# Linear attention with slots and a gated MLP: the middle chunk's products with states in the other quarters of the array, behind the first link; the first expert layer's blocks in the order of use

## The chip, the cores and the metric

The kernel is one program on one core of one Trainium2 chip. The core has a matrix engine (TensorE; PE in the profile, its weight loads PEld), a vector engine (VectorE, DVE), a scalar engine (ScalarE, ACT), a third elementwise engine (GpSimd, POOL) and a sync engine (SP) that issues most transfers. Each works through its own instructions in order, and they wait for one another by semaphores. Matrix products land in PSUM, here in banks of 512 float32 numbers for each of 128 partitions; all other data stand in SBUF.

The metric is the device time of one run in microseconds (us). Before the change the median of three runs is 389.02 us (388.72 to 393.24).

## What is computed

Three layers follow each other: a linear attention with decay, a soft mixture of experts with 32 slots, and a gated MLP.

```python
for t in range(S):                                   # B, H, S, D = 4, 8, 768, 48
    state = alpha[:, :, t, :, None] * state + np.einsum('bhd,bhe->bhde', k[:, :, t], v[:, :, t])
    y[:, :, t] = np.einsum('bhd,bhde->bhe', q[:, :, t], state)
...
logits = x @ phi                                     # x: 3072 x 384, 32 slots
slot_input = softmax(logits, axis=0).T @ x
slot_out[e] = np.maximum(slot_input[e] @ w1[e], 0.0) @ w2[e]      # 8 experts, 384 -> 1024 -> 384
x = softmax(logits, axis=1) @ slot_out
...
g = x @ w_gate                                       # 384 -> 1536 -> 384
out = (g * sigmoid(g) * (x @ w_val)) @ w_out
```

## The kernel before

**The attention.** The 768 positions of a pair of heads (a unit; there are 16) are cut into six chunks of 128. A step works on half a unit, so there are 32 steps g = 0 to 31; h = g % 2 tells the half, c = 0, 1, 2 the chunk in it. The two heads stand in partitions 0 to 63 and 64 to 111. I call a step with h = 1 long and one with h = 0 short, after their times in the profile. A step of the loop in `fast` (L628 on) issues, for the matrix engine and in this order:

- the first link (`emit_st`, L402): the state at a chunk's end is the scaled sum of the chunk's own contribution and the state before. The matrix engine adds the earlier state to the contribution in PSUM by a product with the identity, and the scalar engine scales the sum and writes the state to SBUF (L404);
- the masked scores of the next half (`emit_s`, L353), then the second link, the transposes of the next half's keys (`emit_kt`, L371) and of the last half's output x (`emit_xt`, L462), and the logits of the last half (`emit_l`, L453);
- the products of this half's queries with the earlier states (`emit_past`, L420), into the bank `y`. A half with h = 0 has them for two chunks, since its first chunk has no state behind it, and a half with h = 1 for three;
- the next half's own contributions to the states (`emit_dh`, L390), into a bank of the pool `m`; where a unit begins, the scalar engine then scales the first of them (the state after chunk 0, `emit_st(g + 1, 0)`);
- the products of this half's values with its masked scores (`emit_ip`, L432), added to the same bank `y`, which one scalar copy (L434) brings to SBUF as x.

Each product is two matmul instructions. Those of the two heads stand in different parts of the array: in `emit_past` head 0 reads partitions 0 to 63 and writes partitions 0 to 63, head 1 reads and writes 64 to 111, so that two of the four quarters of the array are in use.

The vector engine makes the decay scans (L307, L314) and the mask of one head (L360), converts parts of a float64 weight to float32 (L253, L257, L261), and runs the short softmax parts of `slot_steps`. GpSimd scales keys and queries (L325) and masks the other head (L363). The scalar engine does the copies out of PSUM.

**The expert layers.** 32 blocks of 768 KB, 16 for each of the two layers, are fetched whole. `Arena` hands out SBUF columns, `loads` sets the order, and `pump` starts the next load when a place is free; in the attention a credit of `RATE` columns a step holds it back. The first layer (L853) runs over four groups: three slices k of the contraction, four experts e. A block before holds one expert's half, all three slices, so each block of a group is released near its end. The second layer is `fc2` (L910), 16 times eight matmuls, each on one block.

**The rest.** `c_stack`, `sw_mul`, `sw_sel` prepare the gated MLP, which runs 72 steps of eleven 512-wide matmuls (L1006, L1007, L1045).

Of the kernel before, what the change touches and what calls it, by code (L numbers as in the profile page):

```python
# [18 lines left out]
CH = 128  # L19
# [15 lines left out]
GV0, RATE = 1, 840  # L35
TINY = 2.0 ** -55
NEAR, ROUND = 31600, 19184
# [55 lines left out]
def attention_slots_mlp(ctx: ExitStack, tc: tile.TileContext, kq, at, vt, phi, w1, w2, wgv, wo, cst, out):  # L93
# [13 lines left out]
    phs = const.tile([112, NU, NSL], F32, name="phs")  # L107
# [33 lines left out]
    def program(general):  # L141
# [16 lines left out]
        zn = {nm: [0] * n for nm, n in (("a", 4), ("p", 5), ("v", 4), ("w", 2), ("x", 2))}  # L158
        zsize = {"a": HW, "p": HB, "v": 288, "w": HW, "x": 384}
        for z in "a0 a1 p2 a2 p3 v0 w0 a3 p4 v1 w1 p0 v2 p1 v3 x0 x1".split():  # L160
            zn[z[0]][int(z[1])] = ar.alloc(zsize[z[0]], 1)
# [32 lines left out]
        for q in range(2):  # L194
            loads += [("w1", (e, hf)) for hf in range(2) for e in range(4 * q, 4 * q + 4)]
# [6 lines left out]
        reserve = [0]  # L202
# [22 lines left out]
        def pump(limit=100):  # L225
            while loads and limit:
                limit -= 1
                nm, i = loads[0]
                o = ar.alloc(size[nm], 0 if nm == "wo" or loads[0] in lasts else 1 if ar.near(BLK) <= reserve[0] else None)
# [150 lines left out]

        def emit_dh(g):
# [4 lines left out]
            dps[g] = psm()  # L386
# [4 lines left out]

        dps = {}
# [15 lines left out]
        yps = {}  # L408


        def emit_past(g):
            n, h = sgs[g]
            q = view(qp[g], 112)
            yps[g] = ps_y.tile([128, 512], F32, tag="y", name="y")
            for c in range(3):
                cc = 3 * h + c
                o = slice(c * CH, (c + 1) * CH)
                for s in range(2) if cc else ():
                    p = slice(0, 64) if s == 0 else slice(64, 112)
                    nc.tensor.matmul(yps[g][p, o], lhsT=gst[n, cc][p, 0:p.stop - p.start], rhs=q[p, o], start=(cc == max(1, 3 * h)), stop=False, skip_group_check=True)  # L420
            del qp[g]
            release(pair.pop(g), z_p, g + 5)

        def emit_ip(g):
            n, h = sgs[g]
            v = view(vv[g]).rearrange("p (c e) -> p c e", e=96)
            ps = yps[g]
            for c in range(3):
                o = slice(c * CH, (c + 1) * CH)
                for s in range(2):  # L430
                    p = slice(0, 64) if s == 0 else slice(64, 112)
                    nc.tensor.matmul(ps[p, o], lhsT=v[:, c, 48 * s:48 * s + p.stop - p.start], rhs=smk[g, s][:, c], start=False, stop=True, skip_group_check=True)  # L432
            xt[g] = (z_x.pop(0), 384)
            nc.scalar.copy(view(xt[g], 112), ps[0:112, 0:384])  # L434
            del smk[g, 0], smk[g, 1], yps[g]
            release(vv.pop(g), z_v, g + 4)
# [8 lines left out]
        def emit_l(g):  # L445
# [5 lines left out]
            for j in range(3):  # L451
                t0 = j * CH
                nc.tensor.matmul(lps[b][32 * j:32 * j + 32, CH * h:CH * h + CH], lhsT=phs[:, u, :], rhs=x[:, t0:t0 + CH], start=(u == 0 and h == 0), stop=(u == NU - 1), skip_group_check=True)  # L453
# [14 lines left out]
        def slot_steps(b):  # L468
# [33 lines left out]

            def part(between=lambda: None):
# [3 lines left out]
                for r in range(2):  # L507
                    if r:
                        between()
                    for u, p, w in pieces:  # L510
                        for j in range(3):
                            nc.tensor.matmul(ps[32 * j:32 * j + 32, 96 * u:96 * u + 96 * w], lhsT=st["et"][:, r, 32 * j:32 * j + 32], rhs=xtok[:, p:p + w, 3 * r + j, :], start=(r == 0 and u == 0), stop=(r == 1), skip_group_check=True)
# [64 lines left out]
        def fast():  # L577
# [14 lines left out]
            keep_warm(10)  # L592
# [15 lines left out]
            keep_warm(4)  # L608
# [10 lines left out]
            keep_warm(6)  # L619
            pend = []  # L620
            credit[0] = 0
            for g in range(NSG):
                n, h = sgs[g]
                nxt = g + 1 < NSG

                emit_st(g, 1 - h)
                if GV0 < g and (g <= 8 or g % 8 not in (3, 4)):
                    conv_y()  # L628
# [22 lines left out]
                if g:  # L651
                    emit_l(g - 1)
                    release(xt.pop(g - 1), z_x, g + 1)
# [7 lines left out]
                emit_past(g)  # L661
# [13 lines left out]
                credit[0] = min(credit[0] + RATE, 2 * BLK)  # L675
# [6 lines left out]
                pump_units()  # L682
            for r in z_t:
# [498 lines left out]
```

## Time and profile before

One profiled execution took 390.72 us, 1.70 us above the median of the runs; its span from the first to the last instruction is 389.0 us. The stages, cut at instructions of the matrix engine, with the busy time of each engine in them:

| stage | from : to, us | PE | DVE | ACT | POOL | DMA, GB/s |
|---|---|---|---|---|---|---|
| start, steps 0 and the beginning of 1 | 0 : 16.98 | 12.11 | 12.66 | 4.42 | 6.45 | 312 |
| attention | 16.98 : 156.06 | 136.63 | 121.12 | 82.33 | 88.29 | 317 |
| last softmax, slot inputs | 156.06 : 162.48 | 5.75 | 2.13 | 2.77 | 0 | 275 |
| first expert layer | 162.48 : 175.63 | 13.15 | 1.91 | 4.76 | 2.55 | 354 |
| second expert layer | 175.63 : 188.88 | 11.59 | 9.14 | 4.02 | 3.55 | 410 |
| preparation of the MLP | 188.88 : 199.24 | 10.36 | 7.69 | 6.26 | 0 | 246 |
| gated MLP | 199.24 : 389.00 | 181.76 | 136.54 | 96.67 | 0 | 55 |

A row of the timeline in the prediction reads: start in us from the span's first instruction, length in us, engine, line, operation, what is written <- what is read, partitions and shape, number of instructions merged; in brackets the idle time of the engine ahead of it and who ended it. A matmul's end is modelled, so stages are measured from start to start. In the rows of waits stand the waiting engine and tile, the one waited for, the total in us, how often, and the longest.

### The profile page before, as it was taken

What the parts mean: (1) busy time and instruction counts of PE and PEld (TensorE: products, weight loads), DVE (VectorE), ACT (ScalarE), POOL (GpSimd) and SP (SyncE); (2) the same over time, 40 slices, a digit from 0 to 9 for tenths busy, and PEclk for the clock granted to TensorE, in tenths of its full rate; (3) what the DMA queues carried; (4) which work ended last, traced back from release to release, by engine and by line L of the source; (5) the groups of instructions that cost most, each with busy time, mean ns of one, the idle gap of its engine ahead of it and who ended that gap; (6) DMA issues with size and microseconds to landing.
All of it is one profiled execution on the core that took longest, in us unless ns stands there. A gap on an engine that the chain in (4) does not pass through costs nothing.

```text
span 389.0 us, 8609 instructions
## 1 busy us (share of the span) xinstructions
PE 371.4 (95%) x3308; PEld 278.9 (72%) x3309; DVE 291.2 (75%) x566; ACT 201.2 (52%) x468; POOL 100.8 (26%) x105
## 2 busy tenths in 40 slices
PE   7799999999999999899899999999999999999992
PEld 3577777777777776434368868888888888888881
DVE  6969997999999973215789987677777867877550
ACT  2256665666456565523376755445455545446441
POOL 3347875685588641010300000000000000000000
PEclk9879999999999999999999999999999999999998
DMA  8969999899899959899900004204204114112002
GB/s 273 352 221 329 373 352 356 289 340 345 275 346 363 336 164 354 298 345 412 401 30 0 3 27 125 73 3 150 71 2 153 40 33 152 37 36 82 3 1 90
DMA packets 28627, 74.25 MB, mean 191 GB/s; under 512 B 3216, under 2 KB 11648, under 8 KB 28576
## 3 DMA queue, kind: packets, MB, share of 16 engines
q1 hardware_dynamic: 28256, 73.27, 53.3%
q8 instruction: 28, 0.46, 0.5%
q10 hardware_dynamic: 272, 0.21, 0.2%
q14 instruction: 23, 0.19, 0.2%
q0 software_dynamic: 48, 0.13, 0.1%
HBM read 68.87 MB, written 4.72 MB: 189 GB/s over the span
## 4 chain that ended last, share of the span: by engine, by line
PE 81%; DVE 6%; DMA 3%; ACT 2%; issue 2%; POOL 1%; SPq 0%; DVEq 0%; ACTq 0%; POOLq 0%
PE m L1045 22%; PE acc L1045 11%; PE s L353 6%; PE y L432 6%; PE y L420 6%; PE s L1006 4%; PE m L402 4%; PE s L1007 4%; PE m L390 3%; PE m L371 3%; PE l L453 3%; DMA near<-w 3%; PE s L853 3%; PE m L462 2%; DVE near L1012 1%
## 5 line engine op out<-in xcount | busy, mean ns | idle before, releaser
L1045 PE MATMUL m<-rnd 128*128 128x512 f32 x432 | 129.2, 389 | 0.0
L1045 PEld LDWEIGHTS m<-rnd 128*128 128x128 f32 x432 | 81.1, 188 | 16.8
L1009 ACT ACTIVATE near<-s 128x512 f32<-128x512 f32 x72 | 43.1, 599 | 79.0 <-PE s L1006 77.3
L1045 PE MATMUL acc<-rnd 128*128 128x512 f32 x216 | 81.1, 392 | 0.7 <-DVE rnd L901 0.7
L325 POOL TENSOR_TENSOR far<-far 112x384 f32<-112x384 f32 x61 | 74.5, 1240 | 8.8 <-DVE far L307 4.7
L1012 DVE TENSOR_TENSOR near<-near,s 128x512 f32<-128x512 f32 x72 | 49.3, 685 | 36.1 <-ACT near L1009 35.9
L1020 DVE TENSOR_TENSOR rnd<-near,rnd 128x512 fp32r<-128x512 f32 x72 | 49.4, 686 | 3.2 <-ACT rnd L1018 3.1
L1045 PEld LDWEIGHTS acc<-rnd 128*128 128x128 f32 x216 | 40.5, 188 | 10.3 <-DVE rnd L901 1.6
L1018 ACT CAST rnd<-near 128x512 fp32r<-128x512 f32 x72 | 44.3, 616 | 0.2 <-DVE near L1012 0.2
L404 ACT ACTIVATE far<-m,tots 112x48 f32<-112x48 f32 x80 | 24.3, 304 | 26.7 <-PE m L402 14.6
L307 DVE TENSOR_TENSOR_SCAN far<-far,r 112x388 f32<-112x388 f32 x32 | 30.8, 962 | 5.1 <-DMA far<-at 2.4
L353 PE MATMUL s<-far 64*128 64x128 f32 x384 | 30.8, 293 | 3.5 <-POOL far L325 2.2
L363 POOL TENSOR_SCALAR_AFFINE_SELECT far<-far 128x384 f32<-128x384 f32 x32 | 20.2, 631 | 47.3 <-ACT far L362 47.3
L1116 DVE TENSOR_REDUCE amm<-near 112x1 f32<-112x768 f32 x32 | 30.3, 946 | 2.5 <-DMA near<-at 2.5
L314 DVE TENSOR_TENSOR_SCAN far<-far,r 112x387 f32<-112x387 f32 x32 | 30.7, 959 | 1.1
L257 DVE SCALAR_TENSOR_TENSOR near<-near 128x384 uint32<-128x384 uint32 x36 | 21.6, 599 | 11.3 <-ACT near L249 10.3
L434 ACT COPY far<-y 112x384 f32<-112x384 f32 x32 | 15.3, 480 | 28.3 <-PE y L432 28.3
L353 PEld LDWEIGHTS s<-far 64*128 64x128 f32 x384 | 24.7, 191 | 6.1 <-POOL far L325 4.5
L432 PE MATMUL y<-far 128*48 128x128 f32 (+1 forms) x384 | 28.9, 276 | 0.0
L1006 PE MATMUL s<-rnd 128*128 128x512 f32 x72 | 28.3, 393 | 0.0
L1007 PE MATMUL s<-rnd 128*128 128x512 f32 x72 | 28.1, 391 | 0.0
L420 PE MATMUL y<-far 48*48 48x128 f32 (+1 forms) x320 | 24.9, 283 | 0.0
(163 smaller groups left out, 493.4 us busy)
## 6 DMA issues: line engine op xcount, KB each, us to landing
near<-w SPq DMA_DIRECT2D x18, 768.0 KB, 7.3
far<-kq SPq DMA_DIRECT2D x32, 384.0 KB, 5.1
far<-w SPq DMA_DIRECT2D x14, 768.0 KB, 6.3
near<-wgv SPq DMA_DIRECT2D x24, 384.0 KB, 5.8
far<-at SPq DMA_DIRECT2D x32, 194.0 KB, 5.0
near<-at SPq DMA_DIRECT2D x16, 339.1 KB, 3.3
far<-vt SPq DMA_DIRECT2D x32, 144.0 KB, 4.6
near<-wo SPq DMA_DIRECT2D x12, 384.0 KB, 8.0
```

What stands on the lines that cost most here:

```text
L307: nc.vector.tensor_tensor_scan(w[:, ::-1], a[:, ::-1], rst[:, ::-1], 0.0, ALU.mult, ALU.add)
L325: eng.tensor_tensor(out=xv, in0=xv, in1=sv, op=ALU.mult)
L353: nc.tensor.matmul(sps[g][s][:, o:o + CH], lhsT=k[64 * s:64 * s + 64, t0:t0 + CH], rhs=q[64 * s:64 * s + 64, t0:t0 + CH], start=True, stop ...
L420: nc.tensor.matmul(yps[g][p, o], lhsT=gst[n, cc][p, 0:p.stop - p.start], rhs=q[p, o], start=(cc == max(1, 3 * h)), stop=False, skip_group_ ...
L432: nc.tensor.matmul(ps[p, o], lhsT=v[:, c, 48 * s:48 * s + p.stop - p.start], rhs=smk[g, s][:, c], start=False, stop=True, skip_group_check ...
L1006: nc.tensor.matmul(pg, lhsT=swk[n][:, 128 * o:128 * o + 128], rhs=ctT[t % 4], start=True, stop=True)
L1007: nc.tensor.matmul(pv, lhsT=swk[n][:, 256 + 128 * o:256 + 128 * o + 128], rhs=ctT[t % 4], start=True, stop=True)
L1009: nc.scalar.activation(sg, pg, AF.Silu)
L1012: nc.vector.tensor_tensor(out=h_, in0=sg, in1=pv, op=ALU.mult)
L1018: nc.scalar.copy(hi, h_)
L1020: nc.vector.tensor_tensor(out=lo, in0=h_, in1=hi, op=ALU.subtract)
L1045: nc.tensor.matmul(p, lhsT=passes[j][0][:, sl], rhs=passes[j][1], start=(f == 0 and j == 0), stop=(f == NF - 1 and j == 2))
```

## The change

In words:

- **Order of the products.** `emit_past(g)` leaves its place behind the logits. The products with the values (`emit_ip`) now come first for a half, and those with the states are issued in the next step, straight behind the first link, for the half before (`emit_past(g - 1)`).
- **Quarters and banks.** The middle chunk (c = 1) writes its two heads crosswise: head 0's result goes to partitions 64 to 111 and head 1's to 0 to 63, which are the array's other two quarters, and into a bank of its own from the pool `m`. Chunks 0 and 2 share the bank `y`. The order of phi's rows (`phs`, now twice as large) and of x's columns (`x_rows`) follows the swap. Two scalar copies (L448, L449) now bring x to SBUF in place of one.
- **The state contributions** (`emit_dh`) move from a bank of `m` of their own to columns 256 to 399 of the bank `y`, so that links, their scaling and the products of chunks 0 and 2 of two neighbouring halves work on one bank.
- **Buffers.** One buffer for x instead of two; `ROUND` 19184 becomes 19056.
- **First expert layer.** Its blocks hold three consecutive (k, e) pieces in the order of use; a block is released after its third product, and `pump` and `get` run after each product.
- **Loads.** When the attention's own loads are all issued, the credit no longer limits the weights; while buffers are wanted on one side of SBUF, loads go to the other. The first conversion of the float64 weight comes one step earlier. The warm-up matmuls write banks of `m`.

The core of the diff:

```diff
         def emit_dh(g):
...
-            dps[g] = psm()
+            dps[g] = new_y()[:, 256:400]
...
+        def swap(c):
+            return int(c == 1 and not general)
+
+        def half(s):
+            return slice(0, 64) if s == 0 else slice(64, 112)
+
+        def y_out(g, s, c):
+            return yps[g][c == 1][half(s ^ swap(c)), CH * (c // 2):CH * (c // 2) + CH]
+
+        def emit_ip(g):
+            cleared = g + 1 < NSG
+            yps[g] = ybank[0] if cleared else new_y(), psm()
+            v = view(vv[g])
+            for c in range(3):
+                for s in range(2):
+                    o = y_out(g, s, c)
+                    e = 96 * c + 48 * s
+                    nc.tensor.matmul(o, lhsT=v[:, e:e + o.shape[0]], rhs=smk[g, s][:, c], start=(c == 1 or c == 0 and not cleared), stop=True, skip_group_check=True)
...
         def emit_past(g):
...
-                    nc.tensor.matmul(yps[g][p, o], lhsT=gst[n, cc][p, 0:p.stop - p.start], rhs=q[p, o], start=(cc == max(1, 3 * h)), stop=False, skip_group_check=True)
+                    o = y_out(g, s, c)
+                    nc.tensor.matmul(o, lhsT=gst[n, cc][half(s), 0:o.shape[0]], rhs=q[half(s), c * CH:(c + 1) * CH], start=False, stop=True, skip_group_check=True)
+            xt[g] = (z_x.pop(0), 384)
+            x = view(xt[g], 112)
+            y, z = yps.pop(g)
+            nc.scalar.copy(x[:, CH:2 * CH], z[0:112, 0:CH])
+            nc.scalar.copy(x.rearrange("p (c t) -> p c t", t=CH)[:, 0::2], y[0:112, 0:2 * CH].rearrange("p (c t) -> p c t", t=CH))
...
                 emit_st(g, 1 - h)
-                if GV0 < g and (g <= 8 or g % 8 not in (3, 4)):
-                    conv_y()
+                if g:
+                    emit_past(g - 1)
+                    if g <= 8 or g % 8 not in (3, 4):
+                        conv_y()
...
-                emit_past(g)
                 if nxt:
                     emit_dh(g + 1)
                     if h:
                         emit_st(g + 1, 0)
                 conv(2)
                 emit_ip(g)
...
-                credit[0] = min(credit[0] + RATE, 2 * BLK)
+                credit[0] = min(credit[0] + RATE, 2 * BLK) if uloads else NEAR
...
+            emit_past(NSG - 1)
...
                 for e in range(4):
-                    r = have["w1", (4 * q + e, hf)]
-                    nc.tensor.matmul(ps[32 * e:32 * e + 32, :], lhsT=st_[:, k, :], rhs=view(r)[:, 512 * k:512 * k + 512], start=(k == 0), stop=(k == 2))
-                    if k == 2:
+                    j, x = divmod(4 * k + e, 3)
+                    r = have["w1", (q, hf, j)]
+                    nc.tensor.matmul(ps[32 * e:32 * e + 32, :], lhsT=st_[:, k, :], rhs=view(r)[:, 512 * x:512 * x + 512], start=(k == 0), stop=(k == 2))
+                    if x == 2:
                         drop(r)
+                get()
+                pump()
```

Where the instructions stand, first on the matrix engine before the change, from a long step's last state contribution over the products with the values and the first link of the short step behind it to that step's scores (a name in brackets is the engine whose semaphore the row waits for):

```order
L390 MATMUL m<-far 48x48
L432 MATMUL y<-far 64x128
L432 MATMUL y<-far 48x128 [waits Pool_49]
L432 MATMUL y<-far 64x128
L432 MATMUL y<-far 48x128
L432 MATMUL y<-far 64x128
L432 MATMUL y<-far 48x128
L402 MATMUL m<-far,cs 64x48 [waits Activation_49]
L402 MATMUL m<-far,cs 48x48
L353 MATMUL s<-far 128x128 [waits DMAHW0_49,DVE_49,Pool_49]
```

The same place after the change, where L396 is `emit_dh`, L433 `emit_ip`, L406 the link and L444 `emit_past`; the products with the states of chunks 1 and 2 follow below the last row, ahead of the scores:

```order
L396 MATMUL y<-far 48x48
L433 MATMUL y<-far 64x128 [waits Activation_49]
L433 MATMUL y<-far 48x128 [waits Pool_49]
L433 MATMUL m<-far 48x128 [waits PE_49]
L433 MATMUL m<-far 64x128
L433 MATMUL y<-far 64x128
L433 MATMUL y<-far 48x128
L406 MATMUL y<-far,cs 64x48
L406 MATMUL y<-far,cs 48x48
L444 MATMUL y<-far 64x128 [waits Activation_49]
L444 MATMUL y<-far 48x128
L444 MATMUL m<-far 48x128
```

Links and contributions now write `y`; the wait for the scalar engine stood at the link and now stands at the first product with the values, and a second one at the first product with the states that writes `y`.

The second place, on the matrix engine behind a long step's first link, where the half before has states for two chunks only; the rows of after:

```order
L406 MATMUL y<-far,cs 64x48
L406 MATMUL y<-far,cs 48x48
L444 MATMUL m<-far 48x128
L444 MATMUL m<-far 64x128
L444 MATMUL y<-far 64x128 [waits Activation_49]
L444 MATMUL y<-far 48x128
L353 MATMUL s<-far 128x128 [waits DMAHW4_49,DVE_49,Pool_49]
```

Here the middle chunk stands ahead of the wait, and chunk 2 behind it.

On the scalar engine the same stretch before the change (L404 scales a state, L374, L466 and L362 copy keys, x and scores, L434 copies x out of PSUM, L249 converts):

```order
L362 COPY far<-s 128x384 [waits Pool_49]
L404 ACTIVATE far<-m,tots 112x48 [waits PE_49]
L434 COPY far<-y 112x384 [waits PE_49]
L404 ACTIVATE far<-m,tots 112x48 [waits PE_49]
L249 ACTIVATE near<-near 128x384 [waits DMAHW7_49,DVE_49,Activation_49]
```

And after it (L408 scales a state, L448 and L449 copy x out of PSUM):

```order
L362 COPY far<-s 128x384 [waits Pool_49]
L408 ACTIVATE far<-y,tots 112x48 [waits PE_49] x2
L448 COPY far<-m 112x128 [waits PE_49,Activation_49]
L449 COPY far<-y 112x2x128 [waits PE_49,Activation_49]
L249 ACTIVATE near<-near 128x384 [waits DMAHW0_49,DVE_49,Activation_49]
```

The copy of x stands behind the scaling for the first link, no longer ahead of it, and is two copies.

More of the change, by code (lines that the diff above doesn't have):

```diff
@@ L106, in attention_slots_mlp @@
     negm = cs[:, 288:289]
-    phs = const.tile([112, NU, NSL], F32, name="phs")
+    phs = const.tile([112, 2, NU, NSL], F32, name="phs")
     tots = const.tile([112, B * NU, NC], F32, name="tots")
@@ L194, in program @@
         for q in range(2):
-            loads += [("w1", (e, hf)) for hf in range(2) for e in range(4 * q, 4 * q + 4)]
+            loads += [("w1", (q, hf, j)) for hf in range(2) for j in range(4)]
         loads += [("w2", (q, k)) for q in range(2) for k in range(8)]
@@ L228, in pump @@
                 nm, i = loads[0]
-                o = ar.alloc(size[nm], 0 if nm == "wo" or loads[0] in lasts else 1 if ar.near(BLK) <= reserve[0] else None)
+                o = ar.alloc(size[nm], 0 if nm == "wo" or loads[0] in lasts else 1 if wants or ar.near(BLK) <= reserve[0] else None)
                 if o is None:
@@ L452, in emit_l @@
                 t0 = j * CH
-                nc.tensor.matmul(lps[b][32 * j:32 * j + 32, CH * h:CH * h + CH], lhsT=phs[:, u, :], rhs=x[:, t0:t0 + CH], start=(u == 0 and h == 0), stop=(u == NU - 1), skip_group_check=True)
+                nc.tensor.matmul(lps[b][32 * j:32 * j + 32, CH * h:CH * h + CH], lhsT=phs[:, swap(j), u, :], rhs=x[:, t0:t0 + CH], start=(u == 0 and h == 0), stop=(u == NU - 1), skip_group_check=True)
         def emit_xt(g, between=lambda: None):
@@ L511, in part @@
                         for j in range(3):
-                            nc.tensor.matmul(ps[32 * j:32 * j + 32, 96 * u:96 * u + 96 * w], lhsT=st["et"][:, r, 32 * j:32 * j + 32], rhs=xtok[:, p:p + w, 3 * r + j, :], start=(r == 0 and u == 0), stop=(r == 1), skip_group_check=True)
+                            nc.tensor.matmul(ps[32 * j:32 * j + 32, 96 * u:96 * u + 96 * w], lhsT=st["et"][:, r, 32 * j:32 * j + 32], rhs=x_rows(p, w, r, j), start=(r == 0 and u == 0), stop=(r == 1), skip_group_check=True)
                 if own:
@@ L1146, in _arrays @@
     vt = c(v.reshape(B, NU, 2, NC, CH, D).transpose(0, 1, 4, 3, 2, 5)).reshape(B, NU, CH, NC * 96)
-    ph = np.zeros((112, NU, NSL), np.float32)
+    ph = np.zeros((112, 2, NU, NSL), np.float32)
     pr = moe_phi.reshape(NU, 2, D, NSL)
     for s in range(2):
-        ph[64 * s:64 * s + 48] = pr[:, s].transpose(1, 0, 2)
-    w1 = c(moe_w1.reshape(NE, 3, 128, 2, 512).transpose(0, 3, 2, 1, 4)).reshape(NE, 2, 128, BLK)
+        for x in range(2):
+            ph[64 * s:64 * s + 48, x] = pr[:, s ^ x].transpose(1, 0, 2)
+    w1 = moe_w1.reshape(2, 4, 3, 128, 2, 512).transpose(0, 4, 2, 1, 3, 5).reshape(2, 2, 4, 3, 128, 512)
+    w1 = c(w1.transpose(0, 1, 2, 4, 3, 5)).reshape(2, 2, 4, 128, BLK)
     w2 = c(moe_w2.reshape(2, 4, 8, 128, DM).transpose(0, 2, 3, 1, 4)).reshape(2, 8, 128, BLK)
```

57 lines of the change are left out of this document (25 added, 32 removed).

## The prediction

> **What bounds the kernel now.** I read the page first, then windows by stage, then the matrix engine's timeline over two neighbouring steps, then the scalar engine's rows that answer it.
>
> ```profile
> span 389.0 us, 8609 instructions
> PE 371.4 (95%) x3308; PEld 278.9 (72%) x3309; DVE 291.2 (75%) x566; ACT 201.2 (52%) x468; POOL 100.8 (26%) x105
> PE 81%; DVE 6%; DMA 3%; ACT 2%; issue 2%; POOL 1%; SPq 0%; DVEq 0%; ACTq 0%; POOLq 0%
> 110.00:120.00 10.00, 10.00 (x164) 7.81 (x160) 9.67 (x21) 6.25 (x19) 9.08 (x8) 1.00 1.02 378
> ```
>
> The last row is one stretch of the attention: PE busy 10.00 us of 10, PEld 7.81, DVE 9.67, ACT 6.25, POOL 9.08, clock 1.00. The matrix engine sets the pace there and carries 81% of the chain. The vector engine stands close behind it: what the matrix engine could save is soon limited by that 9.67, while a longer matrix-engine step meets no such limit.
>
> The matrix engine's timeline from a long step's scores (the link ahead of them belongs to the same step) over a short step to the next scores:
>
> ```profile
> 72.18 0.94 PE L353 MATMUL s<-far 64*128 64x128 f32 x12
> 73.05 0.31 PE L402 MATMUL m<-far,cs 64*64 64x48 f32 x4
> 73.30 0.51 PE L371 MATMUL m<-cs,far 112*128 112x112 f32 x3
> 74.02 0.42 PE L453 MATMUL l<-far,phs 112*32 112x128 f32 x6
> 74.37 0.87 PE L420 MATMUL y<-far 64*64 64x128 f32 x12
> 75.16 0.49 PE L390 MATMUL m<-far 128*64 128x48 f32 x11
> 75.47 0.28 PE L432 MATMUL y<-far 128*48 128x128 f32 x1
> 76.31 0.31 PE L402 MATMUL m<-far,cs 64*64 64x48 f32 x4
> 76.55 0.94 PE L353 MATMUL s<-far 64*128 64x128 f32 x12
> 78.29 0.42 PE L453 MATMUL l<-far,phs 112*32 112x128 f32 x6
> 78.64 0.65 PE L420 MATMUL y<-far 64*64 64x128 f32 x8
> 79.22 0.43 PE L390 MATMUL m<-far 128*64 128x48 f32 x8
> 79.44 0.88 PE L432 MATMUL y<-far 128*48 128x128 f32 x12
> 80.25 0.31 PE L402 MATMUL m<-far,cs 64*64 64x48 f32 x4
> 80.49 0.38 PE L353 MATMUL s<-far 64*128 64x128 f32 x2
> ```
>
> From start to start a long step takes 76.55 - 72.18 = 4.37 us, a short one 80.49 - 76.55 = 3.94, a pair 8.31. In a step the link takes 0.24 (76.31 to 76.55), the products with the states 0.79 for three chunks (74.37 to 75.16) and 0.58 for two (78.64 to 79.22), so 0.21 for a chunk more. From the contributions to the products with the values it is 0.31 in a long step (75.16 to 75.47), and those take 0.84 (75.47 to 76.31). Nothing waits in this stretch.
>
> How fast the scalar engine answers the matrix engine, and the reverse:
>
> ```profile
> 73.42 0.30 ACT L404 ACTIVATE far<-m,tots 112x48 f32<-112x48 f32 x1 [0.22 <-PE m L402]
> 75.77 0.30 ACT L404 ACTIVATE far<-m,tots 112x48 f32<-112x48 f32 x1 [0.75 <-PE m L390]
> 155.53 0.48 ACT L434 COPY far<-y 112x384 f32<-112x384 f32 x1 [1.56 <-PE y L432]
> 156.06 0.31 PE L453 MATMUL l<-far,phs 112*32 112x128 f32 x3 [0.33 <-ACT far L434]
> ```
>
> A link started at 73.05 and its scaling, on an idle scalar engine, at 73.42: 0.37 later, and it takes 0.30. Contributions started at 75.16 and their scaling at 75.77: 0.61 later. The last two rows give the way back: the copy ends at 156.01, the matmul starts at 156.06, 0.05. In the kernel before, both scalings run beside other work of the matrix engine: the one of 75.77 ends at 76.07, beside the products with the values, ahead of the link of 76.31 that needs it.
>
> **The change, part by part.** The decisive thing is that links, their scaling and the products of chunks 0 and 2 now share one bank, and the built program waits for the scalar engine's read of the bank before the matrix engine writes it again. The two waits are in the rows of the order.
>
> *Behind the first link.* The matrix engine starts the link, and may go on with bank `y` 0.37 + 0.30 + 0.05 = 0.72 later. Middle-chunk products fit into that time in a long step, where they stand ahead of the wait; in a short step they stand behind the waiting chunk 0. A long step has chunk 2 left, 0.58 - 0.21 = 0.37, so link to scores 1.09 in place of 0.24; a short step has chunks 0 and 2 with the middle one beside them, 0.58, so 1.30. What goes is the old place: 0.79 in the long and 0.58 in the short step. Net: long 1.09 - 0.24 - 0.79 = +0.06, short 1.30 - 0.24 - 0.58 = +0.48. Queued behind the waiting row are the scores, on which both masks and the scans' consumers hang, so nothing overtakes.
>
> *In the other quarters.* No trace row has all four quarters at work. Three column strips do work together (78.29 to 78.64 for three logits products, 0.35), and the two diagonal quarters do. Bounds for the middle chunk in a short step: 0 and 0.21. I take 0, by the strips. The Trainium skill, TensorEngine Tiling (Array Packing), section Tiling Modes, says that the tiles of a 64 by 64 tiling operate independently, loads and matmuls in parallel; by it the cost would be the lower bound, 0. At the upper bound 0.21 for each of 15 short steps, 3.1 us, come on top.
>
> *Ahead of the products with the values.* In a long step they must wait until the first state is scaled out of the same bank: 0.61 + 0.30 + 0.05 = 0.96 from the contributions' start in place of 0.31, +0.65. Bounds: 0 if the scaling came in time, 0.65 by the row; and it can't come in time, since it starts only when the contributions are done.
>
> *A pair of steps* so costs 0.06 + 0.48 + 0.65 = +1.19 us. Steps 2 to 29 are 14 pairs: +16.7. Step 30, short: +0.5.
>
> *The beginning and the end.* Step 1 runs at a low clock and loses its own products with the states, and its products with the values wait:
>
> ```profile
> 20.99 1.47 PE y L420 x11
> PE m L402 <- ACT far L404: 2.1, 4, 0.6
> 152.78 0.31 PE L402 MATMUL m<-far,cs 64*64 64x48 f32 x4 [0.55 <-ACT far L404]
> ```
>
> -1.5 for the first, +0.8 for the second (0.65, stretched by the clock): -0.7. In the other waits of the second row (2.1 us in four, of which 0.55 is the third row's, in step 31) the scalar engine had the slot exponentials ahead of a link's scaling; with longer steps the vector engine's maximum is there earlier and x's copy no longer stands ahead. I take half of 1.55 back: -0.8, between -1.55 and 0. Step 31 has no scores to cover the copies of x: the second link waits for them, and the last products with the states come behind the products with the values. I estimate +0.6, from 0 to +1.2 (two round trips of 0.5).
>
> *Two copies for one* cost the scalar engine perhaps 0.2 a step; at 6.25 of 10 busy that is covered, as are the vector engine's and GpSimd's work, which gain slack from longer steps. If that cover went, the copy ahead of the transposes of x would come late, but the scores stand between.
>
> *The expert layers.*
>
> ```profile
> PE so L910 <- DMA near<-w: 1.7, 2, 1.1
> 183.88 1.14 DVE L943 TENSOR_SCALAR rnd<-near 128x256 fp32r<-128x256 f32 x4
> 186.19 0.85 PE L910 MATMUL so<-near 128*32 128x384 f32 x8 [0.60 <-DMA near<-w]
> 186.49 2.58 DVE L770 COPY near<-ct 128x512 f32<-128x512 f32 x3
> 188.10 0.85 PE L910 MATMUL so<-near 128*32 128x384 f32 x8 [1.05 <-DMA near<-w]
> 188.88 0.33 PE L774 MATMUL m<-cs,near 128*128 128x128 f32 x1
> ```
>
> Before, the last blocks of the second layer are waited for, 1.65 us. Blocks released after their third product, and loads no longer held back at the attention's end, bring them some microseconds earlier, so this wait goes. What is late next is the vector engine's first copy L770 (three in 2.58 from 186.49, so the first ends near 187.35), which the transposes at 188.88 need and which hangs on the twelfth block, not the last. The gain is the smaller one, 188.88 - 187.4 = 1.5. The first layer's 96 matmuls stay as they are: 0.
>
> *Sum*, on the profiled 390.72 us: +16.7 + 0.5 - 0.7 - 0.8 + 0.6 - 1.5 = +14.8, 405.5. The median of the runs is 1.70 lower: 389.02 + 14.8 = 403.8.
>
> **The rivals.**
> *Faster: the answer comes in time.* If the scalar engine's answer needed no longer than the matrix engine's own work, link to scores would be 0.24 + 0.21 in a long and 0.24 + 0.42 in a short step, and no wait would stand ahead of the values: 0.45 + 0.66 against 0.24 + 0.79 + 0.24 + 0.58, -0.74 a pair, -10.4 in all. The vector engine at 9.67 of 10 lets at most about 3.3% of 139 us through, 4.6. With the expert term: 389.0 - 6.1 = 383. It decides where the answer takes under 0.24 us from the link; the rows say 0.72. Chance 5%. The Trainium skill, PSUM — Partial Sum Buffer, Terms, calls a matrix-engine write and a scalar-engine read of one bank and quadrant at once an error; no run here shows it, but by it the wait can't be left out, and the sum stays at 403.8.
> *The quarters don't overlap* (the change does not do what it says): +3.1, 407. For it: no row shows four. Against: strips and diagonals overlap. Chance 10%.
> *Half of the waits is hidden.* If the wait ahead of the values were covered, as by a scalar engine that starts before all contributions stand, a pair costs +0.54, 14 pairs 7.6, and the whole is 389.0 + 7.6 - 1.9 = 395. Against it: 75.77 shows an idle scalar engine that waited for L390. Chance 10%.
> *The vector engine already sets the pace*, and the matrix engine's longer steps fall into time that it loses anyway: 389 to 392. Against it: the matrix engine is busy 10.00 of 10. Chance 4%.
>
> **How the numbers follow.** Forecast 403.8 us with 71%; its own bounds are 0.65 and 0.48 each off by 0.1 (3 us over 14 pairs), the ends 0.6 and 0.8: 399.5 to 408. To hold 8 in 10 the range takes in the quarters' case above and part of the half-hidden one below: 397 to 409. About 2% (7.8 us) is what a measurement of this kernel tells from no change: 396.8 and 381.2. Slower: forecast 71, quarters 10, and 3 of the half-hidden case: 84%. Within 2%: 7 + 4 of those, 2 of the faster rival: 13%. Faster: 3%.
>
> **What would show it.** In the profile after: pairs of scores 9.5 us apart; L444 with idle time of about 0.4 ended by L408, and L433 in long steps with about 0.6 ended by L408; in each step link to scores near 1.1 and 1.3; the vector engine's share of an attention window down to about 8.5; in short steps 12 instructions of L444 in no longer than 0.58; L910 without a wait for the weights, and the transposes L774 behind L770. I am wrong if L408 starts less than 0.3 after its link, if L433 starts beside the contributions as before, or if scores still lie 8.3 us apart.

## The result, and the profile after

The changed kernel takes 415.55 us in the median of four runs (411.12 to 429.22), where the kernel before, on the same chip, takes 388.87; the ratio is 1.0562, 95% interval 1.0478 to 1.0647. The forecast was 403.8, range 397 to 409: the direction was right, the loss too small. The four runs differ mostly by the clock that the matrix engine was granted on average, 0.986, 0.974, 0.963 and 0.927 for 411.12, 413.16, 417.93 and 429.22 us, and the ratio is of the two faster runs alone.

The profiled run is that of 413.16 us. From its page, the span, the busy engines, the granted clock in 40 slices and the chain that ended last; then, from the windows by stage, the same stretch of the attention as before (PE, PEld, DVE, ACT, POOL busy, clock, DMA share, GB/s):

```profile
span 411.4 us, 8732 instructions
PE 375.6 (91%) x3308; PEld 276.3 (67%) x3309; DVE 288.9 (70%) x566; ACT 205.8 (50%) x500; POOL 94.0 (23%) x105
PEclk8996999999999996999999999999999999999997
PE 68%; DVE 8%; ACT 6%; issue 2%; DMA 1%; ACTq 0%; DVEq 0%
110.00:120.00 10.00, 8.38 (x127) 6.26 (x129) 7.88 (x19) 4.21 (x15) 4.34 (x5) 1.00 0.63 208
```

The matrix engine, busy 10.00 of 10 before, is now busy 8.38, and the scalar engine's share of the chain went from 2% to 6%. Two slices inside the attention show a clock of 0.6: that is new, and no term of the prediction speaks of it.

The matrix engine's timeline over a pair of undisturbed steps, from scores to scores:

```profile
77.55 0.94 PE L353 MATMUL s<-far 64*128 64x128 f32 x12
...
80.67 0.25 PE L406 MATMUL y<-far,cs 64*64 64x48 f32 x2
...
81.39 0.43 PE L444 MATMUL y<-far 64*64 64x128 f32 x4 [0.27 <-ACT far L408]
81.75 0.94 PE L353 MATMUL s<-far 64*128 64x128 f32 x12
...
83.95 0.55 PE L396 MATMUL y<-far 128*64 128x48 f32 x12
84.91 0.43 PE L433 MATMUL y<-far 128*64 128x128 f32 x4 [0.41 <-ACT far L408]
...
85.70 0.31 PE L406 MATMUL y<-far,cs 64*64 64x48 f32 x4
86.42 0.32 PE L444 MATMUL y<-far 64*64 64x128 f32 x2 [0.41 <-ACT far L408]
...
87.00 0.38 PE L353 MATMUL s<-far 64*128 64x128 f32 x2
```

All three waits are where the prediction put them. Link to scores takes 1.08 us (80.67 to 81.75) and 1.30 (85.70 to 87.00), contributions to values 0.96 (83.95 to 84.91), and the pair 87.00 - 77.55 = 9.45, where 9.50 was forecast and 8.31 was measured before. The idle time ahead of the values is 0.41, where the prediction looked for about 0.6; from start to start the time is as forecast. In what follows step k is the stretch from the scores of half k, which the loop issues in its step k - 1, to the scores of the next half; undisturbed, an even one takes 5.25 us and an odd one 4.20, in place of 4.37 and 3.94.

What the prediction did not have is in the waits (waiting engine and tile, the one waited for: total, times, longest), and in the scalar engine's timeline at the steps 4 and 28:

```profile
PE y L444 <- ACT far L408: 11.1, 31, 0.6
PE y L433 <- ACT far L408: 7.7, 15, 0.9
PE y L396 <- ACT far L374: 2.9, 4, 1.3
ACT near L249 <- DMA near<-wgv: 5.0, 4, 1.9
```

```profile
28.20 0.57 ACT L249 ACTIVATE near<-near 128x384 f32<-128x384 f32 x1 [1.24 <-DMA near<-wgv]
...
28.86 0.42 ACT L374 COPY far<-m 128x336 f32<-128x336 f32 x1
...
156.02 0.36 ACT L552 ACTIVATE ct<-ct 128x192 f32<-128x192 f32 x1 [0.56 <-DVE ct L551]
156.29 0.28 ACT L408 ACTIVATE far<-y,tots 112x48 f32<-112x48 f32 x1
```

The conversion L249 waits for its block from memory, and behind it in the scalar engine's queue stands the copy of the key transposes (L374) that the contributions (L396) need: the wait named "ACT far L374" is one for memory. L552, the exponential of the combine weights, waits for the vector engine with a state's scaling L408 behind it; in steps 12, 20 and 28 the wait ahead of the values is 0.95 us for that, not 0.41.

Now the clock, in windows cut where the granted clock changes (same columns as above):

```profile
28.43:31.84 3.41, 1.92 (x38) 1.26 (x32) 3.24 (x9) 2.11 (x7) 1.80 (x2) 1.00 1.02 368
31.84:35.25 3.41, 3.41 (x31) 2.76 (x32) 2.79 (x7) 1.39 (x4) 0.98 (x2) 0.50 0.73 241
35.25:38.67 3.42, 3.42 (x38) 2.43 (x37) 2.15 (x7) 1.13 (x3) 1.78 (x3) 0.50 0.55 207
...
52.32:55.73 3.41, 2.21 (x40) 1.65 (x40) 3.31 (x7) 1.59 (x6) 2.33 (x3) 1.00 0.95 316
55.73:59.14 3.41, 3.41 (x57) 2.64 (x55) 3.24 (x10) 3.06 (x10) 1.59 (x2) 1.00 0.83 258
...
154.72:158.13 3.41, 2.07 (x36) 1.44 (x30) 2.77 (x8) 1.59 (x6) 2.31 (x3) 1.00 0.78 309
158.13:161.55 3.42, 3.40 (x30) 2.76 (x31) 1.06 (x3) 0.92 (x3) 0.00 (x0) 0.50 0.76 237
```

A window of 3.41 us with the matrix engine busy 1.92 or 2.07 us, 56 and 61%, is followed by half clock, which lasts for two windows each time (to 38.67 and to 164.96); one with 2.21, 65%, is not. The two low windows are those with the extra waits of steps 4 and 28. The same wait of 0.95 us stands in steps 12 and 20 too, and there no window falls below 2.44: where a wait lies in its window decides as well.

The Trainium skill, TensorE: Matmul & The Clock Gate, section "What's actually happening", has the free-running window of about 3.4 us and the half rate after an idle window: the length agrees, but these windows were more than half busy. The same page of the Trainium skill, section "A second HAM failure mode: psum-queue depth-cycling", tells of another kernel in which frequent short idle times between groups of matmuls made the clock go back and forth. Here the short waits on the bank alone (0.27 and 0.41 us in the rows above) did not do it, as experiment 6 shows; with one longer wait in the window they did.

### The profile page after: what moved, and what is told of

Its sections match the earlier page's. It is cut to its first block, busy times and chain, and to the rows that moved or that the text cites. A ratio compares the mean times of both kernels' runs of the same rounds, so it can differ in the third digit from the quotient of the medians.

```text
span 411.4 us, 8732 instructions
## 1 busy us (share of the span) xinstructions
PE 375.6 (91%) x3308; PEld 276.3 (67%) x3309; DVE 288.9 (70%) x566; ACT 205.8 (50%) x500; POOL 94.0 (23%) x105
## 4 chain that ended last, share of the span: by engine, by line
PE 68%; DVE 8%; ACT 6%; issue 2%; DMA 1%; ACTq 0%; DVEq 0%
PE m L1073 21%; PE acc L1073 10%; PE s L353 5%; PE s L1034 4%; PE s L1035 3%; PE y L433 3%; PE y L444 3%; PE s L880 3%; PE y L406 2%; ACT far L408 2%; PE m L371 2%; PE so L938 2%; PE l L468 2%; DVE near L1040 2%; DVE rnd L1048 1%
## 5 line engine op out<-in xcount | busy, mean ns | idle before, releaser
L325 POOL TENSOR_TENSOR far<-far 112x384 f32<-112x384 f32 x61 | 68.0, 1134 | 6.6 <-DMA far<-kq 3.8
L408 ACT ACTIVATE far<-y,tots 112x48 f32<-112x48 f32 x80 | 23.9, 299 | 49.6 <-PE y L406 47.3
L433 PE MATMUL y<-far 128*48 128x128 f32 (+1 forms) x256 | 28.5, 288 | 7.7 <-ACT far L408 7.7
L444 PE MATMUL y<-far 64*64 64x128 f32 (+1 forms) x192 | 18.2, 296 | 11.1 <-ACT far L408 11.1
L253 DVE TENSOR_SCALAR near<-near 128x384 uint32<-128x384 uint32 x36 | 12.6, 349 | 18.9 <-DMA near<-wgv 9.6
```

What stands on the lines that cost most here:

```text
L325: eng.tensor_tensor(out=xv, in0=xv, in1=sv, op=ALU.mult)
L408: nc.scalar.mul(gst[n, cc][:, 0:48], ps, tots[:, n, cc:cc + 1])
L433: nc.tensor.matmul(o, lhsT=v[:, e:e + o.shape[0]], rhs=smk[g, s][:, c], start=(c == 1 or c == 0 and not cleared), stop=True, skip_group_ch ...
```

## The experiments

Theory: the steady loss is the two waits on one bank, which the prediction had; the rest comes from waits in the scalar engine's queue that the change makes worse, and from half-clock windows that these start. Rivals: the new order or the quarters themselves cost; the windows come by themselves; the expert layers lose. All times are medians of the runs, ratios are to the kernel before. Of each kernel one run has a trace, and the readings of steps and windows are from that.

**1. A bank of their own for contributions and links.**

```diff
-            dps[g] = new_y()[:, 256:400]
+            dps[g] = ps_d.tile([128, 512], F32, tag="d", name="d")
...
-            yps[g] = ybank[0] if cleared else new_y(), psm()
+            yps[g] = new_y(), psm()
```

Bank `m` has two buffers instead of three during the attention.

> The changed kernel with one thing undone: the state contributions and links have a bank of their own again (d), so neither the products with the states nor those with the values share a bank with what the scalar engine scales. To make room, bank m has two buffers in place of three during the attention; order, other quarters and first expert layer stay as changed. Theory A (the loss is the two waits for the scalar engine in each pair of steps): link to scores 0.45 us in a long step and 0.66 in a short one, nothing waits ahead of the values, a pair of steps falls from 9.45 us to between 8.31 (the kernel before) less 0.74 and the vector engine's 8.05: about 8.05, 14.5 pairs give -20; and with the matrix engine busy again the half-clock windows inside the attention go (-7 us by the steps they stretch): about 385 us. Rival B (the loss is the new order or the other quarters, not the bank): a pair stays above 9 us and the time above 403. Rival C (two buffers of m bring waits of their own): waits for bank m at the transposes of x, time in between, 388 to 400.

394.74 us (389.1 to 398.09), ratio 1.0036 (0.998 to 1.0092): not to be told from the kernel before. In its timeline the pair from 77.64 to 85.29 takes 7.65 us and nothing waits in it; so the waits on the bank cost 9.45 - 7.65 = 1.80 us a pair (the prediction's rows gave 1.93), and without them the change would save 0.66 a pair. Theory A holds for the step, where the pair is even shorter than its 8.05, and rival B falls. But the total stays 10 us above A's 385:

```profile
40.55 0.77 PE L397 MATMUL d<-far 128*64 128x48 f32 x11 [2.02 <-ACT far L375]
55.83 0.43 PE L397 MATMUL d<-far 128*64 128x48 f32 x8 [2.02 <-ACT far L375]
```

```profile
36.93:40.34 3.41, 1.60 (x22) 1.01 (x18) 1.75 (x5) 0.92 (x3) 1.40 (x2) 1.00 0.95 328
40.34:43.75 3.41, 3.20 (x40) 2.71 (x40) 3.31 (x8) 1.48 (x6) 2.50 (x3) 0.50 0.66 263
```

The conversions' wait for memory is longer here, 2.02 us twice, each of them followed by half clock (the rows show the first). Waits for a buffer of `m`, rival C, are not among the long ones.

**2. Chunks in the order 1, 0, 2** in both groups of products:

```diff
-            for c in range(3):
+            for c in (1, 0, 2):
```

> The changed kernel with the order of chunks 1, 0, 2 in place of 0, 1, 2 in both groups of products, so that the middle chunk, whose bank is not the one waited for, is computed while the scalar engine answers. Theory A (both waits have a fixed end, the answer of the scalar engine): a short step's link to scores falls from 1.30 to 1.09 us, the values after the wait in a long step take 0.28 less, a pair falls from 9.45 to about 8.97, 15 pairs give -7: 406 us if the half-clock windows stay, 398 if they go. Rival B (the matrix engine's own work sets the steps and the waits are only where its idle time shows): the pair stays at 9.45, 411 to 413 us.

405.9 us (404.56 to 409.59), ratio 1.0409 (1.0298 to 1.0519). The pair takes 9.23, 0.22 less, where A had 8.97. That the time is A's 406 is chance: A had it for windows that stay, and in the profiled run no half clock is left between the beginning and the end of the MLP. Half of the expectation was wrong:

```profile
82.24 0.49 PE L396 MATMUL y<-far 128*64 128x48 f32 x11
...
83.20 0.65 PE L433 MATMUL y<-far 128*64 128x128 f32 x8 [0.17 <-ACT far L408]
83.78 0.25 PE L406 MATMUL y<-far,cs 64*64 64x48 f32 x2
...
84.50 0.65 PE L444 MATMUL y<-far 64*64 64x128 f32 x8 [0.27 <-ACT far L408]
85.08 0.49 PE L353 MATMUL s<-far 64*128 64x128 f32 x4
```

The values after the wait take 0.58 us (83.20 to 83.78) in place of 0.79 (84.91 to 85.70), 0.21 less where A had 0.28. Link to scores stays at 1.30 (83.78 to 85.08): eight instructions after the wait take the 0.58 that twelve took (86.42 to 87.00), so the middle chunk in the other quarters had cost nothing there, and doing it earlier saves nothing.

**3. Fillers in the waits**: matmuls whose results nobody reads.

```diff
+                    nc.tensor.matmul(p[0:96, 256:384], lhsT=ident[:, 0:96], rhs=mask, start=False, stop=True, skip_group_check=True)
```

> The changed kernel with matmuls that compute nothing needed put into the two waits: one 128x128 by 128 columns ahead of the products with the states, two ahead of the products with the values in long steps, written to unused columns of the logits' bank. Theory A (the half-clock windows follow a stretch of some 3.4 us in which the matrix engine is busy under two thirds): the stretches stay above 70% busy, no window of clock 0.5 inside the attention, the pair stays at 9.45 us or up to 0.1 more, and the time falls by what the windows cost in the profiled run, about 6 to 8 us: 405 to 407, with little spread between runs. Rival B (the windows have another cause, such as heat or power from more work): the windows stay or increase, 411 us or more, and the spread stays.

411.65 us (409.54 to 411.74), ratio 1.0527 (1.0431 to 1.0623). From its page and its windows:

```profile
PEclk9999999999999999999999999999999999999998
110.00:120.00 10.00, 9.64 (x137) 7.18 (x131) 7.61 (x18) 3.97 (x13) 4.67 (x6) 1.00 0.71 228
50.99:54.41 3.42, 2.20 (x32) 1.70 (x32) 3.25 (x9) 2.07 (x7) 1.83 (x2) 1.00 0.90 300
```

No window at half clock is left inside the attention, the mean clock of the four runs is 0.986 to 0.995 in place of 0.927 to 0.986, and they lie within 2.2 us instead of 18: more work, and a higher clock, so that rival B falls, although the time is one that it named. The lowest window, 2.20 of 3.42 or 64% (a conversion's wait without a filler), starts none. The time missed A's 405 to 407, and the ratio does not tell it from the changed kernel's 1.0562: the fillers lengthen the pair by 0.14 (5.39 + 4.20), 2 us in all, the scores of step 2 start at 18.42 in place of 16.96, and the conversions' waits stay.

**4. The middle chunk in the same quarters as the others** (`swap` returns 0).

> The changed kernel with the middle chunk in the same quarters as the others, all else as changed. Theory A (the quarters overlap without cost): the short step's products with the states, after the wait, take 0.79 us in place of 0.58, the products with the values stay at 0.84, the short step is 5.46 us in place of 5.25, 15 of them give +3: about 414 to 416 us with the same number of half-clock windows. Rival B (the other quarters bring nothing here): the steps stay at 5.25 and 4.20 us.

416.88 us (415.44 to 423.83), ratio 1.0657 (1.0563 to 1.0751), an interval that overlaps the changed kernel's, so that the step tells more than the total.

```profile
87.29 0.31 PE L406 MATMUL y<-far,cs 64*64 64x48 f32 x4
88.01 0.43 PE L444 MATMUL y<-far 64*64 64x128 f32 x4 [0.41 <-ACT far L408]
...
88.80 0.94 PE L353 MATMUL s<-far 64*128 64x128 f32 x12
```

Link to scores takes 1.51 (87.29 to 88.80) in place of 1.30, and in the other step 1.08 as before. So in the changed kernel the middle chunk in the other quarters overlaps fully, worth 0.21 where the loop's step is short: the prediction's value 0 for their cost is shown, and its rival falls.

**5. Conversions from the third step on**, as in the kernel before; **6. and the exponential of the combine weights a step later**.

```diff
-                    if g <= 8 or g % 8 not in (3, 4):
+                    if g > 1 and (g <= 8 or g % 8 not in (3, 4)):
```

```diff
-                nc.scalar.activation(ct, ct, AF.Exp)
...
+            def l_exp():
+                ct = ct_all[:, NC * b:NC * b + NC, :]
+                nc.scalar.activation(ct, ct, AF.Exp)
...
-            return [peak, exps, keep, e_tok, part, l_tok, c_norm]
+            return [peak, exps, keep, e_tok, part, l_tok, l_exp, c_norm]
```

> The changed kernel with the scalar engine's part of the conversions beginning in the step after the first two, as in the kernel before, instead of one step earlier; all else as changed. Theory A (started a step earlier, a conversion stands in the scalar engine's queue ahead of the copy of the keys' transposes and waits there for its block from memory): the waits of 0.68 and 1.32 us ahead of the contributions in steps 4 and 8 go, 2.0 us, and the half-clock window that the first of them starts goes with it (3.7 us): 407 to 411 us. Rival B (the blocks come late whatever the step): the two waits stay, 411 to 413 us.

> As the one before, and the exponential of the combine weights is taken a step after its maximum and difference, so that it stands no longer ahead of a state's scaling. Theory A (the half-clock windows follow stretches that a further wait pushes under about two thirds busy; without the further waits the steady steps alone, some 85% busy, start none): no window of clock 0.5 between the second and the last step, the wait ahead of the values in steps 12, 20 and 28 falls from 0.95 to 0.41 us (-1.6 in all), together with the conversions about 402 to 406 us, and the runs lie closer together than those of the changed kernel. Rival B (the windows come by themselves): windows inside the attention stay, and the spread of the runs too.

The first takes 408.63 us (404.8 to 416.53), ratio 1.0415 (1.033 to 1.0501), the second 403.37 (403.31 to 404.69), ratio 1.0358 (1.0304 to 1.0411). The waits of the first, and the clock and the waits of the second:

```profile
PE y L396 <- ACT far L374: 0.5, 1, 0.5
```

```profile
PEclk9999999999999999999999999999999999999997
PE y L444 <- ACT far L408: 11.1, 31, 0.6
PE y L433 <- ACT far L408: 6.1, 15, 0.4
```

Without the conversions' waits (2.9 to 0.5 us) the time falls, but the runs still spread over 12 us. In the profiled one the exponential's waits of 0.95 us start no window; half clock stands at its beginning, from 16.61 on for four windows, and stretches steps 2 and 3 by 5.4 us (8.49 + 6.39 in place of 9.45). That the exponential's waits make the spread is therefore not shown.

Without both kinds of waits, those ahead of the values are 0.4 at the longest, half clock shows nowhere before the end of the MLP, and four runs lie within 1.4 us, 0.4 us from the forecast of 403.8. That it is as close as 0.4 is in part luck: the span of the profiled run, 401.58, is 12.6 longer than before, and the kernel before has 2.95 us of half clock in its step 2 that this run has not; without them the growth is 15.5, where 14.8 was forecast.

The waits on the bank are all there (11.1 us in 31, as in the changed kernel): in this trace they alone start no window, and in those of the changed kernel and of experiment 4 the windows inside the attention stand where a further wait comes on top of them.

**7. The first expert layer's part alone**, in the kernel before; **8. and the change without it**.

> The kernel before with the second half of the change alone: the first expert layer's blocks in the order of use, released after their third product, the wants taken during that layer, and loads not held back once the attention's own loads are out. Theory A (the term of the prediction): the waits for the weights ahead of the second layer's products go and the transposes behind them wait for the vector engine's copy instead, -1.5 us: about 387.5 where the kernel before has 389.0. Rival B (the freed space is used late, or the loads collide with the attention's): 388 to 391, no difference that shows.

> The changed kernel with the second half of the change undone: the first expert layer's blocks in the old order, released together, the wants taken behind the layer's group, loads held back as before. Theory A (the prediction's expert term, the new order brings the second layer's blocks earlier): the waits for weights ahead of the second layer's products are back, between the first layer's end and the transposes behind the second lie 13.8 us in place of 12.3, +1.5 us. Rival B (the blocks come in time because the slower attention leaves more time for loads): the stage stays at 12.3 us and the time at that of the changed kernel.

The first takes 388.91 us (387.39 to 390.72), ratio 0.9983 (0.9952 to 1.0014): no difference, as its rival B has it. The second takes 419.96 (407.81 to 424.96) at mean clocks from 0.942 to 0.993, so only its stage can be read. From the first layer's end to the transposes behind the second it is 13.77 us in the kernel before, 15.20 with the new part alone, 12.32 in the changed kernel, 12.72 without the part. Waits for weights, of the kernel before plus the part, and of the change without it:

```profile
PE so L914 <- DMA near<-w: 2.9, 3, 1.1
```

```profile
PE so L934 <- DMA near<-w: 0.8, 1, 0.8
```

Of the 1.45 us that this stage gained, about 0.4 hangs on the new block order; the other 1.05 is there without it, as rival B of the second has it; its reason, that the longer attention leaves more time for the loads, is likely but has no run of its own. The part alone, in the kernel before, makes the stage longer. Why it does is not settled: the loads stand against the attention's own there, but buffers differ as well.

**9. Own bank with both edits of 6**; **10. the same with the old first layer; 11. the same as 9 with the middle chunk in the same quarters.**

> The kernel with a bank of its own for contributions and links, and both edits of the kernel before the last one: conversions from the third step on, the exponential a step later. Theory A (what held the own bank's kernel at 389 to 398 us although its steady pair takes 7.65 us is waits of the scalar engine's queue, 0.69 and twice 2.02 us for conversions and some 4 us at the slots): the three waits ahead of the contributions go, about 384 to 389 us, at or below the kernel before. Rival B (memory and GpSimd, busy all the time in its steady steps, set the pace): the time gained shows as waits for GpSimd's scaling or for loads, 389 to 394 us.

> The fastest kernel so far (own bank, conversions from the third step, exponential a step later) with the second half of the change undone. Its attention is the shorter one, so its loads have the least time. Theory A (the new order brings the blocks earlier): waits for weights ahead of the second layer's products of 2 us or more, 387 to 390 us. Rival B (they come in time in any case): no such wait, 383 to 387 us as with the new order.

> The fastest kernel so far with the middle chunk in the same quarters as the others. Theory A (in a step without waits the other quarters save what the middle chunk costs, 0.21 us in each of the two groups where they overlap): the pair rises from 7.65 us towards the 8.31 of the kernel before, by 0.4 to 0.7 us, 14 pairs: 388 to 393 us where matrix engine sets the pace. Rival B (GpSimd, memory or the scalar engine already set the pace of most steps): the time stays at 383 to 388 us.

They take 385.36 us (382.99 to 387.21), ratio 0.9888 (0.9841 to 0.9934); 386.62 (381.75 to 392.39), ratio 0.9885 (0.9834 to 0.9936); and 386.86 (384.43 to 389.74), ratio 0.992 (0.9873 to 0.9968). So the kernel of 9, with the new order of products, a bank that is not shared, and the scalar engine's queue without its long waits, is faster than the kernel before by 1.1%: clear of the noise, but under 2%. What the exponential's later place alone would bring in the kernel before was not run, so the gain is that of the whole.

With the old layer one wait for weights of 1.0 us is back, where A had 2 or more, but the total cannot be told from that of 9. In the kernel with the same quarters the pair takes 8.07 us (4.26 + 3.81): the quarters are worth 0.42 a pair where nothing waits, and the order 0.24 against the 8.31 of the kernel before. Of the 14 x 0.42 = 5.9 us only 1.5 show in the medians, and the intervals of the two ratios overlap. From the windows and the timeline of 9:

```profile
24.00:50.00 26.00, 24.30 (x405) 18.59 (x402) 24.92 (x57) 17.67 (x54) 26.00 (x19) 1.00 1.01 372
84.72 0.31 PE L407 MATMUL d<-far,cs 64*64 64x48 f32 x4 [1.16 <-ACT far L409]
```

GpSimd is busy 26.00 of 26 us from 24 to 50, and the DMA share is 1.01. The matrix engine's only waits in that stretch are four for GpSimd's scaling, 1.6 us in all, so there GpSimd holds it up, as rival B has it, though the total is A's. At the slots the link still waits up to 1.16 us for a scaling that stands behind the slot exponentials.

## Why the prediction was right and where it failed

The growth of the profiled span from 388.99 to 411.43 us, 22.4, against the terms of the sum. As in the prediction, steps 30 and 31 are those of the loop here, from the first link of one to that of the next; the conversions and the half clock stand in the stretches numbered as above.

| term | forecast | measured | from |
|---|---|---|---|
| 14 pairs | +16.7 | +16.0 | 14 x (9.45 - 8.31) |
| step 30 | +0.5 | +0.5 | 4.42 (169.86 to 174.28), before 3.93 (147.99 to 151.92) |
| beginning | -0.7 | -0.2 | scores of half 2 to the link of the loop's step 2: 3.95, before 7.08, less the 2.95 that stand in the half-clock row |
| waits at the slots | -0.8 | +0.4 | -1.2 in the kernel of experiment 6, then 3 x 0.54 for L552 |
| conversions a step earlier | no term | +2.5 | steps 4, 8, 10: 0.68 + 1.38 + 0.46 |
| half-clock windows | no term | +3.1 | 6.0 in steps 4, 5, 28, 29, less the 2.95 of one in step 2 before |
| step 31 to the first expert layer | +0.6 | +0.6 | 11.12 (174.28 to 185.40), before 10.56 (151.92 to 162.48) |
| expert layers and the rest | -1.5 | -0.5 | -1.45 at the transposes, 0.5 lost behind them, 0.5 after the last matmul |

The first link of step 31, before and after:

```profile
151.92 0.31 PE L402 MATMUL m<-far,cs 64*64 64x48 f32 x4
```

```profile
174.28 0.25 PE L406 MATMUL y<-far,cs 64*64 64x48 f32 x2
```

The sum is 7.6 us short of the 22.4. Of these the clock has 3.1, the earlier conversions 2.5, the slots 1.2, the expert layers 1.0 and the beginning 0.5; the pairs took 0.7 less than forecast.

- **The two waits on the bank**: right in mechanism, place and size. Link to scores 1.08 and 1.30 (1.09 and 1.30 forecast), contributions to values 0.96 (0.96). Experiment 1 shows that the bank causes them, experiments 2 and 4 that they end with the scalar engine's answer: whatever the middle chunk does, it comes 0.72 behind the link, and in experiment 2 as before 0.96 behind the contributions.
- **The quarters**: the cost of 0 was right (experiments 2 and 4), and so were the sizes of steps 30 and 31; the second link of step 31 waits 0.54 us for the copy of x, as said.
- **The beginning**: the prediction took its step 1 at the low clock of the run before, in which the products with the states take 1.5. In the run after that step has the full clock, and without the 2.95 us of half clock what is left is -0.2. In the kernels of experiments 1, 2 and 5 half clock begins there again, at 16.45, 16.34 and 16.61; no run tells what decides it.
- **The waits at the slots**: this step failed in its sign. It said that with longer steps the vector engine's maximum is there earlier. That part did come, -1.2 once the exponential was out of the way; but the bank makes the matrix engine wait for every scaling, also where another instruction of the scalar engine stands ahead of it, and L552 does.
- **The earlier conversion** was read in the diff and given no price. It is an instruction moved ahead in the queue of the engine on whose answers the kernel had just been made to wait; experiment 5 took its waits away, but for 0.5 us at the beginning.
- **The sum took the clock of the run before as given.** It is the largest of the terms that are missing. The growth of 22.4 on the median of 389.0 before gives 411.4, outside the range; without the clock's 3.1 it would be 408.3, without the conversions' 2.5 it would be 408.9, both inside. At 8.38 of 10 busy a few tenths of further waiting, where they fall into one window, are enough for half clock, and by the mean clocks of the four runs, 0.927 to 0.986, how much of it comes differs from run to run; the median lies at 415.55 with two runs at 0.963 and 0.927, of which there is no trace. Experiments 3 and 6 show the cause from both sides, filled waits and removed ones. With both waits of the queue removed the forecast is met, in part by luck, as said there.
- **The expert layers**: the second layer's weights came in time and the transposes wait for the vector engine's copy, as said (the first row). Two things failed: the next products wait for that engine again (0.52 us in the second row), and the reason given, the blocks' release and order, is only the smaller part of the gain (0.4 of 1.45, experiments 7 and 8).

```profile
210.34 0.66 PE L798 MATMUL m<-cs,near 128*128 128x128 f32 x4 [0.43 <-DVE near L794]
212.79 2.36 PE L1003 MATMUL sw<-near 128*32 128x256 f32 x32 [0.52 <-DVE near L993]
```

- **The faster rival** had the right gain without the waits, -0.74 a pair (0.66 measured in 1). Its limit, the vector engine at 8.05 us a pair, was wrong: pairs of 7.65 ran with that engine. In the kernel of experiment 9 waits for GpSimd and, at the slots, the scalar engine's order are left, and the gain is 1.1%.

## What to carry to other kernels

When a change puts two engines on one PSUM bank, price the round trip at every use, and then go through the queue of the answering engine: each instruction in it that waits for something else has now become a wait of the matrix engine. When a matrix engine that was busy throughout becomes busy for five sixths, ask which window of 3.4 us has the longest waits; the clock may turn a few tenths of a microsecond there into three. A bank of its own, paid with a buffer elsewhere, took away the loss of 5.6% (ratio 1.0036); together with the two edits of the scalar engine's queue it is a gain of 1.1%.

## What the hardware showed that I had not expected

The clock fell to half after windows of 3.41 us that were far from idle. In the attention of these kernels every window of up to 61% busy was followed by half clock (1.60, 1.92 and 2.07 us in the rows above; 1.68 and 1.99 in the kernel of experiment 4, below), and 2.20 and 2.21 were not. The border isn't sharp by this measure: in the kernel of experiment 9 a window with 2.23 was followed by half clock, and in that of experiment 10 one with 2.20.

```profile
28.73:32.14 3.41, 1.99 (x35) 1.35 (x34) 3.05 (x9) 2.03 (x6) 1.31 (x2) 1.00 0.89 298
69.69:73.10 3.41, 1.68 (x30) 1.26 (x30) 3.34 (x8) 2.12 (x7) 1.79 (x3) 1.00 0.86 211
```

```profile
83.26:86.67 3.41, 2.23 (x33) 1.47 (x31) 3.25 (x9) 3.20 (x12) 1.35 (x2) 1.00 1.00 376
86.67:90.08 3.41, 3.41 (x44) 2.75 (x41) 3.31 (x8) 1.20 (x5) 2.63 (x3) 0.50 0.88 318
```

Outside the attention this measure doesn't hold: in the kernel of experiment 7 a window in the second expert layer, 183.30 to 186.71, had 1.62 of 3.41 and kept the full clock. What the chip counts is therefore not the busy time of the profile itself, and no run here tells what it is.

The windows of one run lie on one grid. The half clock inside the attention begins at 31.84 and at 158.13 us in the changed kernel, 126.29 apart, and at 32.14 and 73.10 in that of experiment 4, 40.96 apart: 37 and 12 times 3.413. So what a wait costs depends on where it falls on that grid.
